# Converting eight weight tiles in pairs and squaring 24 units in pairs, with a new order of the first stage

## The chip, the core and the metric

One core of a Trainium2 chip. The metric is the device time of one execution in microseconds (us). In every matmul below TensorE (PE) runs at one of two clocks, 1.2 or 2.4 GHz; the profile gives the granted share, where 1.00 is 2.4 GHz.

## The reference

An attention layer feeds two dense layers, all in float32 (the weights arrive as float64):

```python
# attention: 2 batches, 8 heads, 768 positions, head size 64
k_sum = k.reshape(B, H, nb, 32, D).max(axis=3)      # one summary key per block of 32
v_sum = v.reshape(B, H, nb, 32, D).mean(axis=3)
scores_l = scale * q @ k^T, kept where |i - j| < 16, else -1e9
scores_s = scale * q . k_sum + log(32)
a = softmax([scores_l, scores_s]);  attn = a @ [v, v_sum]
# 1536 tokens, 512 wide
h = x @ w_in;   x = relu(h)**2 @ w_out              # w_in 512x2048, w_out 2048x512
h = x @ w_in2;  g = h if h>=1, 0 if h<=-1, else (h+1)**2/4;  out = g @ w_out2
```

## The kernel before

Every engine's program is written out by hand. `PLAN` is one string of words such as `H0`, `dq1` or `wh1a`; each word is a step, a number and, where there is a choice, an engine (`a` ScalarE = ACT, `v` VectorE = DVE, `g` GpSimd = POOL). The steps are emitted in that order, so each engine runs its own steps in the order in which they stand in the string, and a step that waits holds up everything behind it on its engine. SyncE (SP) issues all loads, also in the string's order.

Attention is cut into 24 pieces, `S0` to `S23` (a piece is 256 query rows of two heads). For a piece: `S` (PE, L611) multiplies queries with the 96 near keys and the 24 block maxima, which `km` (DVE, L599) makes of a loaded key tensor (`kl`, L582); `M` (DVE, L619) adds the mask and finds the largest; `E` (ACT, L625) is the exponential; `Q` and `R` (DVE, L628, L632) are sum and reciprocal; `N` (L637, POOL or DVE) scales; `T` (PE, L642) transposes, into banks 5 to 7 and later into bank 7 alone; `to` (L645) copies out; `O` (PE, L653) multiplies with the values; `oh` and `ol` (L662, L666) write the result as a high and a low float32r half, `xh` and `xl`. `v`, `vk`, `f` and `vf` make and place the block means of the values.

The weights come as float64. `wl` (L203) loads a tile of 128x512 of them as pairs of 32-bit words; `dl`, `dq` (ACT, L209, L214), `dr`, `ds`, `dt` (DVE, L216 to L220) and `da` (POOL, L223) rebuild a float32 high part `fx` and a rest `fr` from the words; `wh` (L237) rounds `fx` to the high half and `wo` (L242) subtracts to get the low half. Tiles 0, 1 and 4, 5 are `w_in`, tiles 2, 3 and 6, 7 are `w_out` of the first group.

The first group of the first dense layer (four blocks of 128 hidden columns) is done in 24 units `H0` to `H23`, one per block of 256 tokens and hidden block. `H` (PE, L282) is 12 matmuls into half a bank; `ha` (L348, L350) is the relu, `hb` (ACT, L361) the square, `hh` (L373) the high half, `hl` (L377) the low half; `Y` (PE, L409) is 12 matmuls with `w_out` that add into the output banks, which `yo` (L420) copies out. Units 0 to 11 all go to the two halves of bank 4 and relu moves them to SBUF (`tm`); units 12 to 23 use the two halves of banks 4 and 3 in place. All other groups (`P...`, `Y24` on, PE L314 and L409) use a scheme of seven block products with 384 columns, whose operand sums are the steps `ua` to `ur` (L498, L524, L526).

```python
def h_bank(n):
    if n < 12:
        return bank[4][:, n % 2 * CH:(n % 2 + 1) * CH]
    return bank[4 - n % 2][:, n // 2 % 2 * CH:(n // 2 % 2 + 1) * CH]
```

Of the kernel before, what the change touches and what calls it, by code (L numbers as in the profile page):

```python
# [66 lines left out]
dr4 S8 dl5 dr5 O4 hb0 M8 T6 hh0a oh4a H1 R7 E8 ol4 N7g M9 to6a O5 ds5 hl0g Q8 T7 oh5a ha1a ol5 S10 to7a dt5 dl4 ds4 O6
wl9 da5 M10 E9 Y0 wl6 wl7 oh6v vf2 E10 R8 ol6 N8g Q9 O7 S11 hb1 Q10 R9 dt4 T8 N9g oh7a ql4 hh1a R10 ol7 H3 wl8 to8a
M11 bl2 wh4a kl7 da4 S12 wh5a E11 T9 M12 N10g H2 km6 E12 wo5g S13 Q11 dq6 hl1v O8 wo4g dq7 R11 ha2v Y1 hb2 dr7 ha3a
hh2a M13 dl6 hl2g H5 hb3 to9v N11g hh3a dl7 ds7 S14 E13 hl3g Q12 T10 H4 dr6 oh8a to10a ol8 R12 M14 N12g T11 ha4a Y2  # L70
Q13 to11a km7 E14 v6 ds6 S15 dt7 ha5a hb4 O9 R13 dt6 hh4a ql5 v7 wh7a Q14 Y3 da6 hb5 bl3 oh9v M15 vl4 da7 H6 ol9 R14
hl4v dq9 wh6v v8 hh5v ha6a O10 N14v hb6 v9 dr9 oh10a H7 ol10 uf0v hl5v v10 hh6v O11 ha7v hl6g wo6v v11 hb7 Y4 N13g
vk7a dq8 vk6v vk4v oh11a vk5a ol11 H8 E15 vf4 wo7g vf3 hh7a Q15 T12 dl9 Y6 to12v ha8a dr8 hl7v T13 R15 ds9 Y7 ds8
to13a ua0v hb8 yo7a N15v O12 ub0v S16 oh12a dt8 S17 uc0g ol12 T14 M16 H9 M17 E16 ug0g Y5 dl8 Q16 yo5a wl10 O13 hh8v
da8 R16 ha9v S19 N16v to14a E17 S18 uh0g T15 M18 H10 hb9 oh13a to15a Q17 E18 dt9 hl8g T16 M19 H11 wl11 to16a ol13 hh9a
R17 N17v O14 hl9g Q18 S21 oh14a ha10a da9 R18 ol14 S20 ui0a O15 E19 M20 uj0g T17 vl5 ha11v Y8 E20 M21 N18g oh15a S23
hb10 ol15 to17a uk0v S22 hh10a O16 LW0 wh9v H13 Q20 oh16a wo9g hb11 R20 E21 ul0v N20g Y9 Q19 wh8a ol16 um0a R19 hh11v
saa2g O17 Q21 T18 wo8v un0g oh17a H14 M22 to18a dq11 hl10v E22 H12 hl11g sab2v ud0a N19g Y10 ol17 ha12a dr11 ha14a
hb12 uo0g dq10 Q22 T19 hb14 Y11 M23 to19a hh12a sac2v yo11a T20 dr10 sad2v Pa0 ha13a R21 R22 N21v E23 N22g O18 hl12
H15 oh18a sh4a ol18 up0g Q23 to20a ds11 hh14a O19 sh5a Y12 ha15a sl5g oh19a hl14 hb13 ol19 ds10 O20 sl4g dl11 T21  # L80
oh20v R23 H18 dt10 dl10 dt11 hb15 to21a H16 N23v wl13 da11 hh13a ol20 wl12 wh10a hl13 O21 hh15a wh11a ue0g hl15 T22
oh21v ha16a Y13 ol21 hb16 wo11v uq0a da10 to22a Y14 ur0v dq13 ha18a dl13 O22 T23 wo10v oh22a dq12 H19 ua1g ol22 to23a
dr12 dl12 ub1g dr13 O23 hh16a H17 oh23a ds12 hl16 ol23 ds13 H20 ha17a uc1v dt12 LS0 ud1a dt13 Y15 ue1g wl14 ha20a hb18
wh12v wl15 hb17 ha19a hh17a Pz0 da12 Pc0 hb19 Ca0v yo15a hl17 uf1v Pb0 da13 ug1v dq14 Pd0 hh18a wo12g H21 hl18 dr14
wh13a Cc0a wo13g H22 ds14 saa3g Y16 sab3v ha22a uh1v hb22 ha24a sac3v ha21v Y17 sad3g hh19a hb20 hl19 sh6a dt14 dq15
H23 sl6g sh7a dr15 ui1a Y18 sl7v hb21 ha23a uj1v dl14 Y19 uk1g wl16 hh21v Vb0 yo19a hh20v da14 hl21 Pf0 hl20 ds15 Y20
ul1v ha25v um1a dt15 dl15 un1g Y21 hh22v hb24 wl17 hb25 uo1v Pe0 wh14v up1g hl22 dq16 hh24v hh25a Pa1 da15 hl24 hb23
hh23a Vc0 Y22 uq1a ha26v ur1g hl23 hb26 hl25 wh15a Y23 dr16 ua2g hh26a Ca1v dq17 hl26 Pd1 ub2v ds16 dt16 Pc1 uc2v
ha28v Pb1 Cc1a dr17 ud2a ds17 yo23a Pg0 ue2g Vb1 hb28 Pf1 uf2g ha27a hh28v wh16a dt17 Pe1 wo14g hb27 hl28 wh17a Y24
hh27a Vc1 hl27 ha30a wo15g ug2v dl16 wl18 Y25 dl17 uh2v ha29a wl19 da17 hb30 da16 Pg1 wo17v Pa2 ha31a hh30a hb31 Y26  # L90
hb29 ui2a hh31a uj2g hh29a hl31 Y27 hl29 uk2g hl30 Ca2a saa4g ul2v Pc2 sab4g ya1 um2a ya0 dq19 un2g Pd2 ya3 sh9a wo16v
# [705 lines left out]
```

## Time and profile before

| | us |
|---|---|
| median of 3 runs (lowest, highest) | 590.32 (587.84, 590.85) |
| the profiled execution | 590.83 |
| its span, first to last instruction | 589.0 |
| PE busy in the span | 572.5 |
| DVE, ACT, POOL busy | 471.0, 375.8, 257.2 |

Busy time is the union of an engine's instructions. PE's ends are modelled, so it can read busy while its pipeline is not full. The chain is the sequence of pieces of work that ended last, followed back from the end; an engine's idle time matters only where it stands on that chain.

### The profile page before, as it was taken

To read this page: it belongs to the slowest core of one execution; us is meant where nothing else is said; L and a number is where in the kernel's file an instruction comes from. 1 tells how busy PE (TensorE), PEld (TensorE's weight loads), DVE (VectorE), ACT (ScalarE), POOL (GpSimd) and SP (SyncE) were. 2 spreads that over 40 slices of the span, in tenths; PEclk is the share of its full clock that TensorE was granted. 3 is DMA by queue.
4 is the path that set the end of the run, shared out by engine and by line. 5 is a ranking of instruction groups with operands and counts; after the bars stand their busy time and mean duration, and the time that the engine had idled before them with its cause. 6 is when DMAs were issued, how large, how long until landed. Compare 5 with 4: busy or idle time off the path is not lost.

```text
span 589.0 us, 11229 instructions
## 1 busy us (share of the span) xinstructions
PE 572.5 (97%) x4272; PEld 531.5 (90%) x4272; DVE 471.0 (80%) x1062; ACT 375.8 (64%) x800; POOL 257.2 (44%) x220
## 2 busy tenths in 40 slices
...
PEclk8888999999999999999999999999999999999999
...
GB/s 336 377 279 288 145 65 92 1 104 76 38 72 75 70 107 83 98 4 118 93 72 30 44 71 2 142 37 108 21 124 0 133 73 51 32 1 1 0 55 160
DMA packets 16529, 54.16 MB, mean 92 GB/s; under 512 B 1724, under 2 KB 2332, under 8 KB 16476
## 3 DMA queue, kind: packets, MB, share of 16 engines
...
q14 instruction: 20, 0.16, 0.1%
...
## 4 chain that ended last, share of the span: by engine, by line
PE 87%; DVE 6%; DMA 4%; ACT 2%; issue 1%; SPq 0%; DVEq 0%; ACTq 0%
PE bank L409 42%; PE bank L314 33%; PE bank L282 5%; DMA raw<-in_wd_dram 3%; PE bank L611 2%; PE bank L653 2%; PE bank L642 1%; PE bank L466 1%; DMA k<-in_kd_dram 1%; DVE s L619 1%; DVE s L637 1%; DVE sm L628 1%; ACT s L625 1%; DVE xl L666 0%; DVE fx L216 0%
## 5 line engine op out<-in xcount | busy, mean ns | idle before, releaser
L223 POOL TENSOR_TENSOR fr<-fx,fr 128x512 uint32<-128x512 uint32 x64 | 85.0, 1338 | 144.6 <-DVE fx L220 95.1
L377 DVE TENSOR_TENSOR gl<-bank,gh 128x384 fp32r<-128x384 f32 (+1 forms) x124 | 65.2, 538 | 16.2 <-ACT gh L373 14.8
L314 PE MATMUL bank<-xh,wih 128*128 128x384 f32 x224 | 75.4, 337 | 0.1
L314 PE MATMUL bank<-xl,wih 128*128 128x384 f32 x224 | 75.1, 335 | 0.0
L409 PE MATMUL bank<-gh,woh 128*128 128x384 f32 (+1 forms) x288 | 66.3, 321 | 0.0
L409 PE MATMUL bank<-gl,woh 128*128 128x384 f32 (+1 forms) x288 | 65.7, 319 | 0.6 <-DVE gl L377 0.6
L409 PE MATMUL bank<-gh,wol 128*128 128x384 f32 (+1 forms) x288 | 65.4, 319 | 0.0
L352 ACT ACTIVATE tm<-bank,bias 128x384 f32<-128x384 f32 x59 | 34.1, 579 | 37.9 <-PE bank L314 25.6
L314 PE MATMUL bank<-xh,wil 128*128 128x384 f32 x224 | 57.1, 335 | 0.0
L314 PE MATMUL bank<-th,wih 128*128 128x384 f32 x168 | 56.7, 337 | 0.1
L314 PE MATMUL bank<-tl,wih 128*128 128x384 f32 x168 | 56.3, 335 | 0.0
L409 PE MATMUL bank<-woh,gh 128*128 128x512 f32 x180 | 55.9, 392 | 0.0
L409 PE MATMUL bank<-wol,gh 128*128 128x512 f32 x180 | 55.9, 391 | 0.0
L409 PE MATMUL bank<-woh,gl 128*128 128x512 f32 x180 | 55.9, 391 | 0.0
L214 ACT ACTIVATE fx<-raw 128x512 f32<-128x512 f32 x64 | 42.5, 668 | 19.6 <-DMA raw<-in_wd_dram 13.4
L369 DVE SCALAR_TENSOR_TENSOR bank<-bank,tm 128x384 f32<-128x384 f32 x64 | 35.5, 560 | 22.4 <-ACT tm L365 15.1
L434 DVE TENSOR_TENSOR acc<-bank,acc 128x384 f32<-128x384 f32 (+1 forms) x81 | 46.7, 601 | 7.3 <-PE bank L409 7.3
L409 PEld LDWEIGHTS bank<-gl,woh 128*128 128x128 f32 x288 | 49.2, 190 | 1.0 <-DVE gl L377 0.9
L373 ACT CAST gh<-bank 128x384 fp32r<-128x384 f32 (+1 forms) x83 | 38.5, 468 | 17.9 <-DVE bank L369 15.3
L409 PEld LDWEIGHTS bank<-gh,woh 128*128 128x128 f32 x288 | 48.9, 189 | 1.0 <-issue 0.4
L409 PEld LDWEIGHTS bank<-gh,wol 128*128 128x128 f32 x288 | 49.4, 191 | 0.0
L209 ACT ACTIVATE fr<-raw 128x512 uint32<-128x512 uint32 x64 | 42.1, 671 | 10.0 <-POOL wil L259 6.5
...
## 6 DMA issues: line engine op xcount, KB each, us to landing
...
```

Source lines behind the costliest of these rows:

```text
L209: A.activation(fr[n % 2], w_raw(n, 0), AF.Copy, scale=2.0 ** -29)
L214: A.activation(f32(x), f32(hi), AF.Abs)
L223: G.tensor_tensor(fr[n % 2], fx[n % 2], fr[n % 2], ALU.add)
L282: PE.matmul(h_bank(n), a, b, start=i == 0, stop=i == len(ops) - 1)
L314: PE.matmul(q_bank(q, role), a, b, start=bool(first and i == 0), stop=i == 5, skip_group_check=not first)
L352: A.activation(a, h, AF.Relu, bias=bias[:, 1:2], scale=-1.0)
L369: V.scalar_tensor_tensor(h, h, 1.0, a, ALU.max, ALU.mult)
L373: cp(e)(hi, h if m else a)
L377: e.tensor_tensor(lo, h if m else a, f32(hi), ALU.subtract)
L409: PE.matmul(ys[j], a, b, start=f == 0 and i == 0 and (n >= 24 or j % 2 == 0), stop=f == GF - 1 and i == 2 and (n >= 24 or j % 2 == 1))
L434: V.tensor_tensor(a, y_bank(g, t, j), a, ALU.add)
L611: PE.matmul(sbank(i, 2 * h + t)[r * 64:r * 64 + 64, 0 if keys else KW:KW if keys else KN], qs[cc % 2][rows, p, j * QT:(j + 1) * QT], b, st ...
```

## The change

Three things. Weight tiles 0 to 7 are converted two at a time: `raw`, `fx` and `fr` become tiles of 1024 columns, and the words `dl`, `dq`, `dr`, `ds`, `dt`, `da` and `wh` with numbers 0 to 3 now mean a pair of tiles (`wo` stays one tile at a time). The 24 units keep their 12 matmuls `H` and `Y` each, but `ha`, `hb`, `hh` and `hl` with numbers 0 to 11 now mean two units with 512 columns, which lie in the two halves of one bank; the pairs of units 0 to 11 all lie in bank 4, the later pairs alternate between banks 4 and 3. And the words of `PLAN` ahead of `Pa2` stand in another order, with some steps on another engine; from `Pa2` on the string is the same, word for word.

```diff
-warm11 kl0 qf0 cl0 kl1 qf1 kl3 wl1 bl0 km0 kl2 wl0 S0 bl1 M0 wl3 E0 km1 S1 ql1 Q0 vl0 M1 wl2 R0 km3 S3 E1 N0g dq1 Q1
+warm11 qf0 kl3 kl0 wl1 kl1 cl0 wl0 qf1 kl2 bl0 km3 ql1 km0 wl2 S0 wl3 km1 S1 bl1 M0 dq0 M1 dl0 S3 dr0 E1 ds0 dt0 E0 km2
...
-        raw = [mp.tile([128, 512, 2], U32, name=f"raw{i}") for i in range(NRAW)]
-        fx = [mp.tile([128, 512], U32, name=f"fx{i}") for i in range(2)]
-        fr = [mp.tile([128, 512], U32, name=f"fr{i}") for i in range(2)]
+        raws = [mp.tile([128, 1024, 2], U32, name="raw0")]
+        fxm, frm = (mp.tile([128, 1024], U32, name=x) for x in ("fx", "fr"))
...
-        gh = [mp.tile([128, TB], F32R, name=f"gh{i}") for i in range(3)]
-        gl = [mp.tile([128, TB], F32R, name=f"gl{i}") for i in range(3)]
-        tm = [mp.tile([128, TB], F32, name=f"tm{i}") for i in range(3)]
+        ghm, glm = (mp.tile([128, 3 * TB], F32R, name=x) for x in ("gh", "gl"))
+        tmm = mp.tile([128, 3 * TB], F32, name="tm")
+        gh, gl, tm = ([x[:, i * TB:(i + 1) * TB] for i in range(3)] for x in (ghm, glm, tmm))
...
         def w_load(n):
-            r = raw[n % (2 * NRAW)] if n < 8 else raw[n % NRAW]
+            r = raws[n // 2 % 2 if n < 8 else 0][:, half(n)]
...
         def w_raw(n, k):
-            return (raw[n % (2 * NRAW)] if n < 8 else raw[n % NRAW])[:, :, k]
+            return raws[n % 2][:, :, k] if n < 4 else raws[0][:, half(n), k]
+
+        def w_tmp(t, n):
+            return t if n < 4 else t[:, half(n)]
 
         def w_low(n):
-            A.activation(fr[n % 2], w_raw(n, 0), AF.Copy, scale=2.0 ** -29)
+            A.activation(w_tmp(frm, n), w_raw(n, 0), AF.Copy, scale=2.0 ** -29)
...
         def w_add(n):
-            G.tensor_tensor(fr[n % 2], fx[n % 2], fr[n % 2], ALU.add)
+            G.tensor_tensor(w_tmp(frm, n), w_tmp(fxm, n), w_tmp(frm, n), ALU.add)
...
         def w_hi(n, e=A):
+            if n < 4:
+                h = w_place(2 * n)[0]
+                cp(e)(h[:, :1024], f32(fxm))
+                return
...
         def h_bank(n):
-            if n < 12:
-                return bank[4][:, n % 2 * CH:(n % 2 + 1) * CH]
-            return bank[4 - n % 2][:, n // 2 % 2 * CH:(n // 2 % 2 + 1) * CH]
+            b = 4 if n < 12 else 4 - n // 2 % 2
+            return bank[b][:, n % 2 * CH:(n % 2 + 1) * CH]
...
-            if n < 24:
-                h = h_bank(n)
-                return h, tm[n % 2][:, :CH] if n < 12 else h, gh[n % 3][:, :CH], gl[n % 3][:, :CH], 0
+            if n < 12:
+                h, ks = bank[4 if n < 6 else 4 - n % 2], half(n)
+                return h, tmm[:, ks] if n < 6 else h, ghm[:, ks], glm[:, ks], 0
...
-                m, hi, lo = 0, gh[n % 3][:, :CH], gl[n % 3][:, :CH]
+                gs = slice(n % 4 * CH, n % 4 * CH + CH)
+                m, hi, lo = 0, ghm[:, gs], glm[:, gs]
...
-        raw += [at.tile([128, 512, 2], U32, name=f"raw{NRAW + i}") for i in range(NRAW)]
+        raws.append(at.tile([128, 1024, 2], U32, name="raw2"))
```

Three places show what the new order moves. The first is the start of ACT's program; before, each conversion step takes one tile (L214, L209, L237), between exponentials (L625):

```order
L625 ACTIVATE s_128<-s_128,sm_137 128x120 x4
L625 ACTIVATE s_129<-s_129,sm_138 128x120 x4
L214 ACTIVATE fx_77<-raw_75 128x512
L209 ACTIVATE fr_79<-raw_75 128x512
L625 ACTIVATE s_131<-s_131,sm_140 128x120 x4
L237 CAST wih_80<-fx_77 128x512
L209 ACTIVATE fr_78<-raw_74 128x512
L214 ACTIVATE fx_76<-raw_74 128x512
L214 ACTIVATE fx_77<-raw_108 128x512
L625 ACTIVATE s_130<-s_130,sm_139 128x120 x4
```

Now two conversions of a pair stand ahead of the first exponential (the exponential is L630 there):

```order
L215 ACTIVATE fx<-raw_74 128x1024
L210 ACTIVATE fr<-raw_74 128x1024
L630 ACTIVATE s_119<-s_119,sm_128 128x120 x4
L630 ACTIVATE s_118<-s_118,sm_127 128x120 x4
L239 CAST wih_77<-fx 128x1024
L630 ACTIVATE s_121<-s_121,sm_130 128x120 x4
L630 ACTIVATE s_120<-s_120,sm_129 128x120 x4
L215 ACTIVATE fx<-raw_98 128x1024
```

So four exponentials instead of three come before ACT turns to the weights a second time, and both tiles of the first pair are through `dq`, `dl` and `wh` by then.

The second place is the first activations on ACT, before with one unit each (L348 relu, L361 square, L373 high half):

```order
L348 ACTIVATE tm_94<-bank_67 128x256
L214 ACTIVATE fx_76<-raw_74 128x512
L645 COPY acc<-bank_70 120x512
L209 ACTIVATE fr_79<-raw_75 128x512
L361 ACTIVATE tm_94<-tm_94 128x256
L373 CAST gh_88<-tm_94 128x256
L662 CAST xh<-bank_69 128x256
```

and now with two units each (L352, L365, L377):

```order
L352 ACTIVATE tm<-bank_67 128x512
L667 CAST xh<-bank_69 128x256
L210 ACTIVATE fr<-raw_74 128x1024
L667 CAST xh<-bank_69 128x256
L365 ACTIVATE tm<-tm 128x512
L650 COPY pt_123<-bank_69 120x512
L377 CAST gh<-tm 128x512
```

Both units of a pair now have to be through PE before the first of the three runs.

The third place is the relu of the second pair, `ha1`, which has moved to DVE (L354, last row but one). Ahead of it stand a `wh` of a pair (L239), a block maximum (L604) and a `wo` that takes its input from POOL's wide add (L247):

```order
L624 ISA s_121,sm_130<-bank_69,cst 128x120
L624 ISA sm_130 128x1
L239 CAST wih_78<-fx 128x1024
L604 TENSOR_REDUCE ks_114<-k_106 128x24
L247 TENSOR_TENSOR wil_80<-fr,wih_78 128x512
L354 TENSOR_SCALAR tm<-bank_67 128x512
L624 ISA s_118,sm_127<-bank_68,cst 128x120
```

Before, DVE's first relu was that of unit 2, and a reciprocal stood ahead of it:

```order
L377 TENSOR_TENSOR gl_92<-tm_95,gh_89 128x256
L632 RECIPROCAL sm_140<-sm_140 128x4
L350 TENSOR_SCALAR tm_94<-bank_67 128x256
L216 TENSOR_SCALAR fx_77<-fx_77 128x512
```

## Rows read from the trace of the kernel before

**Rows 1.** The page's parts 1 and 2: busy time, granted clock by slices of 14.7 us

```profile
PE 572.5 (97%) x4272; PEld 531.5 (90%) x4272; DVE 471.0 (80%) x1062; ACT 375.8 (64%) x800; POOL 257.2 (44%) x220
...
PEclk8888999999999999999999999999999999999999
```

**Rows 2.** Busy time by stretch: length, PE, PEld, DVE, ACT, POOL (instructions), clock, DMA, GB/s

```profile
20.00:40.00 20.00, 15.36 (x294) 13.19 (x287) 16.73 (x74) 18.48 (x50) 11.29 (x10) 0.83 0.94 334
...
0.00:45.64 45.64, 36.32 (x611) 27.45 (x614) 35.68 (x151) 33.01 (x85) 19.69 (x25) 0.85 0.90 331
45.64:84.50 38.86, 37.42 (x560) 34.54 (x560) 29.95 (x110) 25.55 (x66) 19.31 (x16) 0.96 0.50 163
84.50:110.00 25.50, 23.58 (x407) 22.23 (x406) 24.51 (x77) 20.39 (x56) 17.98 (x15) 1.00 0.25 74
110.00:165.40 55.40, 55.40 (x470) 53.64 (x470) 50.42 (x93) 39.11 (x91) 38.70 (x30) 1.00 0.21 70
0.00:165.40 165.40, 152.72 (x2041) 137.85 (x2042) 140.56 (x429) 118.06 (x296) 95.69 (x85) 0.95 0.47 164
```

**Rows 3.** PE's waits from 165.4 us to the end: total, times, longest

```profile
PE bank L409 <- DVE gl L377: 0.6, 1, 0.6
```

**Rows 4.** The chain in order of time (start, length, what), up to 46 us

```profile
6.70 11.45 DMA raw<-in_wd_dram
...
26.39 1.25 ACT s L625 x4
...
33.76 1.17 PE bank L282 x5
...
39.06 1.43 PE bank L282 x12
...
45.02 0.61 PE bank L653 x16
45.64 0.69 PE bank L611 x32
```

**Rows 5.** ACT by shape up to 165.4 us: count, busy, mean ns, idle before

```profile
L625 ACT ACTIVATE s<-s,sm 128x120 f32<-128x120 f32 x96 | 29.7, 389 | 9.4 <-DVE sm L619 9.3
...
L214 ACT ACTIVATE fx<-raw 128x512 f32<-128x512 f32 x18 | 12.0, 673 | 4.6 <-DMA raw<-in_wd_dram 2.2 <-POOL fr L223 1.4 <-issue 1.1
...
L237 ACT CAST wih<-fx 128x512 fp32r<-128x512 f32 x6 | 3.6, 622 | 0.4 <-DVE fx L220 0.4
...
L645 ACT COPY pt<-bank 120x512 f32<-120x512 f32 x17 | 10.0, 586 | 1.6 <-PE bank L642 1.6
...
L361 ACT ACTIVATE tm<-tm 128x256 f32<-128x256 f32 x12 | 5.0, 414 | 3.0 <-DVE tm L350 3.0
...
L524 ACT CAST th<-acc 128x768 fp32r<-128x768 f32 x3 | 2.5, 824 | 0.0
...
L524 ACT CAST th<-tm 128x384 fp32r<-128x384 f32 x4 | 2.1, 516 | 1.4 <-DVE tm L498 1.4
```

**Rows 6.** The same of DVE and of POOL

```profile
L216 DVE TENSOR_SCALAR fx<-fx 128x512 f32<-128x512 f32 x18 | 10.8, 610 | 0.4 <-ACT fx L214 0.4
...
L377 DVE TENSOR_TENSOR gl<-bank,gh 128x256 fp32r<-128x256 f32 x12 | 4.9, 416 | 1.0 <-ACT gh L373 0.9
...
L377 DVE TENSOR_TENSOR gl<-bank,gh 128x384 fp32r<-128x384 f32 x5 | 2.7, 548 | 0.0
...
L223 POOL TENSOR_TENSOR fr<-fx,fr 128x512 uint32<-128x512 uint32 x18 | 24.5, 1368 | 15.4 <-DVE fx L220 12.9 <-ACT xh L662 1.7 <-ACT fr L209 0.8
...
L498 POOL TENSOR_TENSOR acc<-acc,xl 128x768 f32<-128x768 f32 x4 | 7.7, 1933 | 5.6 <-PE bank L653 5.6
```

**Rows 7.** DVE and POOL in order of time, around 67 us and 85 us

```profile
67.41 0.65 DVE L637 TENSOR_TENSOR s<-s,sm 128x480 f32<-128x480 f32 x1
...
86.30 1.89 DVE L637 TENSOR_TENSOR s<-s,sm 128x480 f32<-128x480 f32 x1
...
85.78 1.89 POOL L498 TENSOR_TENSOR acc<-acc,xl 128x768 f32<-128x768 f32 x1
```

More of the change, by code (lines that the diff above doesn't have):

```diff
@@ L67 @@
[L67 to L91, printed above, removed]
@@ L162 @@
-za2 zd2
+warm11 qf0 kl3 kl0 wl1 kl1 cl0 wl0 qf1 kl2 bl0 km3 ql1 km0 wl2 S0 wl3 km1 S1 bl1 M0 dq0 M1 dl0 S3 dr0 E1 ds0 dt0 E0
+km2 da0 wh0a v0 Q1 S2 M3 v1 R1 ql2 M2 E3 S5 N1v vl0 Q0 E2 wo0g Q3 T1 R0 R3 v2 M5 dq1 N3v v3 to1a S7 E5 dr1 vl1 wo1g v4
+T3 Q2 v5 Q5 to3a vk2v M7 N0g S4 vk3a vk0a vk1a dl1 S9 R2 ds1 N2g T0 vf0 M4 f0a to0a cl1 f1a E4 T2 wl5 R5 dt1 O0 N5g
+to2a O1 vf1 E7 S6 Q4 R4 wl4 O2 M6 N4g oh0a kl5 O3 oh2a ql3 wh1v ol2 S8 kl6 da1 oh1a vl2 ol0 E6 T4 wl7 M8 kl4 S10 to4a
+Q7 oh3a O4 wo2g ol1 E8 Q6 T5 R6 ol3 H1 oh4a N6g R7 to5a ol4 Q8 dq2 O5 M9 N7g T6 oh5a M10 H0 wo3g to6a R8 ol5 E10 dr2
@@ new lines @@
+N8g T7 S11 km5 to7a ha0a O6 ds2 T8 vf2 oh6a dl2 ol6 dt2 wl6 O7 oh7a hb0 wl8 ol7 H2 da2 M11 vl4 wh2v kl7 H3 to8a vl3
+hh0a bl2 km4 E9 wl9 wo4v S12 ha1v O8 hb1 M12 hl0g H4 Q9 E12 wo5g Q10 H5 R9 km6 dq3 N9g Q12 E11 Y0 dr3 ha2a ds3 T9 hh1a
+R10 H6 oh8v to9a hl1g ol8 dl3 Q11 O9 R11 R12 N10v S13 N11g T10 dt3 H7 to10a oh9v wh3a da3 M13 T11 ha3a Y2 ol9 to11a
+E13 v6 wo7g hb3 Q13 v7 S14 dq9 wo6g bl3 O10 N12g ql4 v8 R13 M14 Y3 oh10a E14 N13v ol10 km7 v9 O11 hh3a uf0v v10 dq8
+v11 hb2 S15 vk4a Q14 hl3g vk7a Y1 vk5v dl9 oh11a R14 ol11 vk6a dr9 vf3 Y6 hh2v ds9 ql5 hl2v M15 vf4 T12 dt9 Y7 ug0v
@@ new lines @@
+ha30a Y25 ha29v hb30 uh2v wo17v Pg1 Pa2 ha31a hh30a hb31 Y26 hb29 ui2a hh31a uj2g hh29a hl31 Y27 hl29 uk2g hl30 Ca2a
+saa4g ul2v Pc2 sab4g ya1 um2a ya0 dq19 un2g Pd2 ya3 sh9a wo16v dq18 Pa3 Cc2a sac4v dr19 Pb2 sad4g ya2 dr18 uo2g Y28
+ha32v ds18 hb32 hh32a Vb2 sh8v sl9v Pf2 sl8g up2v Pe2 dl18 Y29 ds19 ha33a dt19 hb33 dt18 uq2a hh33a hl32 ur2g wl20
+dl19 Y30 hl33 wh18a Vc2 wl21 da18 Ca3v wh19a ha34v da19 hb34 Y31 wo19g ya5 ya4 Pg2 hh34v wo18g dq21 ya6 hl34 Pd3 ha35v
+dr21 hb35 Pc3 ds21 dq20 ha36v Pb3 dt21 Cc3a hb36 ya7 hh35a Y32 Vb3 dl21 wh21v dr20 dl20 wl23 da21 hh36a hl36 Pe3 ds20
@@ L235, in w_hi @@
         def w_hi(n, e=A):
+            if n < 4:
+                h = w_place(2 * n)[0]
+                cp(e)(h[:, :1024], f32(fxm))
+                return
             h, l, o, c = w_place(n)
-            cp(e)(h[:, o:o + c.stop - c.start], f32(fx[n % 2][:, c]))
+            cp(e)(h[:, o:o + c.stop - c.start], f32(fxm[:, half(n)][:, c]))
         def w_lo(n, e=G):
@@ L241, in w_lo @@
             d = slice(o, o + c.stop - c.start)
-            e.tensor_tensor(l[:, d], f32(fr[n % 2][:, c]), f32(h[:, d]), ALU.subtract)
+            e.tensor_tensor(l[:, d], f32(frm[:, half(n)][:, c]), f32(h[:, d]), ALU.subtract)
         def w_sum(p, k, e=G):
-            a, b = f32(fr[0]), f32(fr[1])
+            a, b = f32(frm[:, :512]), f32(frm[:, 512:])
             lo, hi = slice(0, 256), slice(256, 512)
@@ L253, in s_hi @@
             p, k = divmod(n, 2)
-            cp(e)(wih[p % 3][:, 1280 - k * 512:1792 - k * 512], f32(fr[k]))
+            cp(e)(wih[p % 3][:, 1280 - k * 512:1792 - k * 512], f32(frm[:, half(k)]))
         def s_lo(n, e=G):
```

163 lines of the change are left out of this document (86 added, 77 removed).

## The prediction, made before the changed kernel ran

> **What bounds it now.** I read the page first, then busy time by stretch, then PE's waits, then the chain. PE is busy 97% of the span and its clock is full from about 60 us on [rows 1], so the question is only where PE loses time. From 165.4 us on it waits 0.6 us in all [rows 3]. That is also where `Pa2` starts, and from `Pa2` on both programs are the same word for word, so those 424 us stay as they are and merely begin earlier or later. Up to 165.4 us PE is idle 165.4 - 152.7 = 12.7 us, and its clock is at 0.95 on average, which is worth some 8 us more [rows 2]. **So about 20 us is the most that the change can win.** Of the 12.7 us, 9.3 lie before 45.64 us, 1.4 up to 84.5 and 1.9 in 84.5 to 110; after that there is none [rows 2].
>
> The reader is to see in the chain who sets PE's pace. At 6.70 us a weight load starts that lands at 18.15; then the chain runs through exponentials on ACT (26.39 us is one of them), and from 33.76 us mostly through PE itself [rows 4]. The stretch 20 to 40 us agrees: ACT 18.5 of 20 us, PE 15.4 [rows 2]. So ACT sets the pace in the first third, DVE later: in 84.5 to 110 us it is busy 24.5 of 25.5 us [rows 2].
>
> **The change, part by part.** *Wide conversions on ACT.* A 512-column step takes 0.67 us [rows 5]. A 1024-column one is not in the trace. Two rows give its growth: 516 ns at 384 columns and 824 at 768, 0.80 ns a column [rows 5], so 0.82 + 256 x 0.80 = 1.03 us at the least; at the most it is twice 0.67 = 1.35, nothing saved. I take 1.10, near the wide rows. The activations of two units (512 columns) cost 0.60, like the 512-column copy (0.586), against 2 x 0.41 [rows 5].
>
> *ACT's work ahead of `O7`.* I take `O7` as a common mark, since PE has done nearly the same before it (12 instead of 11 `S`, one `T` more, no `Y0`; 0.5 us less in all). In ACT's order stand ahead of it: one `E` fewer, 1.24 us (29.7 us for 24 pieces); 6 wide conversions for 12 narrow ones, 8.1 - 6.6 = 1.5; one wide `wh` of 1.05 for four of 0.62, 1.4 (the other pair's has gone to DVE); one wide activation for four narrow steps, 1.0; one copy more, -0.6; the rest -0.1 [rows 5]. Sum: **4.4 us less on ACT.**
>
> *What may not arrive.* ACT now begins with `dq0`, which needs two weight tiles; before, the exponentials of pieces 0 and 1 came first. And `dq1` waits for the fourth tile, which is now behind 5888 KB of loads instead of 5376; at the 331 GB/s of this stretch [rows 2] that is some 1.6 us later than 18.15, so about 19.7. Ahead of `dq1` ACT has work for 2.2 + 5.0 + 1.05 us from about 10 us on, so it is idle some 1.5 us at 18 us; before, the chain too waited for this tile. I put 0.6 us of that against the 4.4, since the chain before waited for this tile as well. Behind it, up to `to4`, which `H1` stands behind, lie 12 us of ACT work (four `E`, four copies, one `dl`, small ones): `H1` starts at about 33.5 us. Up to `to7` another 6.5 us: `O7` ends near 41 against 45.6 (45.02 + 0.61 [rows 4]), with 0.5 us less done. **Stage 1: -3.5 to -4; I take -3.8.** The cover of this sum is that DVE does not take over: its work ahead of `O7` falls too, by about 3 us (one `Q`, one `km`, one `N` fewer, 9 wide for 17 narrow steps).
>
> *From there to `Pa2`.* PE has the same work, 114 us in both. DVE gets lighter by pairing: 24 conversion steps of 0.61 us (less where POOL is quiet) become 12 wide ones, and 30 activation steps of 0.42 become 15 of 0.69 (0.416 at 256 columns, 0.548 at 384, so 1.03 ns a column [rows 6]): together -4 to -7 us. But the new order gives it 26 steps which POOL and ACT had (high halves of `O`, operand sums, low halves) and takes 11 away; at 0.42 to 0.95 us a step that is some +14 - 8 = +6 to +8. So DVE's work up to `Pa2`, 140.6 us of 165.4 [rows 2], changes by -3 to +4, while the time for it gets shorter. The 1.9 us that PE lost in 84.5 to 110 may go (the units' steps there are half as many); against it, a new wait of about 2 us at the second pair (rival C's place). **Stage 2: 0, between -4 and +6.** POOL loses 15 steps; nobody on the chain waits for it, so that counts only through the next point.
>
> *DVE against POOL.* A scaling step `N` takes DVE 0.65 us at 67.41 and 1.89 us at 86.30, where a POOL sum runs from 85.78 to 87.67 [rows 7]. The Trainium skill, "SBUF — State Buffer", section "Who interferes with whom", says that DVE and POOL share one port pair and that whoever comes second is blocked for the whole instruction of the other; the trace agrees, 0.65 against 1.89 us. A wide POOL add is not in the trace; from 1368 ns at 512 columns and 1933 at 768 it is about 2.5 us, at the most 2.74 [rows 6]. Four of these hold DVE longer at a time, but 10 us in place of 11; with 15 POOL steps fewer this speaks for the lower end of DVE's -3 to +4.
>
> **The sum**, against the profiled execution's 590.8 us (the median of the runs is 590.3): -3.8 + 0 + 0 gives 587.0.
>
> **Rivals.** *B, the relief is hidden or given back:* ACT waits for weights as much as it saves, or DVE, without slack in 45 to 165 us, returns the 4 us. For it: DVE was busy 24.5 of 25.5 us in 84.5 to 110 [rows 2] and gets up to 4 us more. Against it: PE never waited after 110 us although DVE was busy 50.4 of 55.4 [rows 2]. Time: 590.8 - 3.8 + 3 = 590.
>
> *C, the one bank of the first pairs:* slower. Pairs 0 to 5 all lie in bank 4, so the next pair's `H` waits until the relu of the last one has read both halves. The relu of pair 1 is on DVE behind a `wo` that needs POOL's wide add; DVE has 40 us of steps ahead of it, so it comes at 45 to 46 us, while PE could be through `H3`, `S12` and `O8` (0.69 and 0.61 [rows 4]) at about 44. That is the 2 us above. If this repeats at `H2`, `H4`, `H6` and `H8` and the clock, which was at 0.83 in 20 to 40 us when PE was idle a quarter of the time [rows 2], falls there as well (an `H` of 1.43 us [rows 4] then takes twice that, three of them +4.3), the stage gives back 4 x 2 + 4.3 = 12: 590.8 - 3.8 + 12 - 2 = 597; half of it gives 593. It decides from about 1.6 us a pair. The Trainium skill, "Perfetto Trace Analysis", section "Optimizing Scalar/DVE Operations", speaks for this case: larger operations help a saturated engine, but where an engine is not saturated and makes others wait, breaking up instructions may let work end sooner. ACT is at 64% over the span but at 92% in 20 to 40 us, so by the rows the first half of the rule holds there.
>
> *D, more than forecast:* ACT ends the first stage earlier and the low-clock stretches shrink with the gaps: up to half of the 20 us, 581.
>
> **Chances.** Forecast with its own range 584 to 588.5: 0.42; D 0.12; B 0.28; C 0.18. Range 581 to 593: it leaves out the far half of C and of D. A measurement tells about 0.5%, 3 us, from no change: under 587.4 is faster, over 593.3 slower. 0.36 of the forecast's 0.42 and D give faster 0.48; B, the rest of the forecast and 0.02 of C give same 0.36; the rest of C is slower, 0.16.
>
> **What would show it.** Right: `O7` ends near 41 us and `H1` starts near 33.5; a wide `dq` near 1.1 us, a wide `da` near 2.5; `Pa2` starts at 161 to 162 us and from there 424 us remain; ACT busy about 105 us up to `Pa2`. Wrong: `O7` not before 44 us (B: look at ACT's wait for `raw`); `O7` early but `Pa2` at 165 (B: DVE on the chain in 60 to 160 us); PE idle or at half clock ahead of `H4` and `H6` (C).

## The result, and the profile after

The changed kernel takes 596.28 us (median of 4 runs, 594.24 to 598.09) against 589.66 of the kernel before, measured beside it: 1.0115 times as long, 95% interval 1.009 to 1.014. Forecast were 587.0 us and faster. The profiled execution takes 596.14 us, 5.3 more than the one before.

Marks on PE split this: `O7` starts at 45.34 us (before 44.95), `Pa2` at 169.38 (before 165.38), and from `Pa2` to the end of the span 424.8 us pass (before 423.7). So stage 1 gives +0.4, stage 2 +3.6, the rest +1.2. By the prediction's own count PE has 0.5 us less to do ahead of `O7` now, so for equal work stage 1 is some 0.9 us late and stage 2 adds some 3.1.

Parts 1 and 2 of the page of the changed kernel:

```profile
PE 571.4 (96%) x4272; PEld 529.0 (89%) x4272; DVE 470.5 (79%) x1051; ACT 365.8 (62%) x750; POOL 243.9 (41%) x205
...
PEclk8699999999999999999999999999999999999999
```

Busy time by stretch, columns as in [rows 2]; the fourth stretch ends where `Pa2` starts:

```profile
0.00:45.64 45.64, 34.16 (x625) 25.11 (x627) 33.13 (x139) 29.40 (x69) 19.29 (x22) 0.81 0.87 312
45.64:84.50 38.86, 36.71 (x609) 33.46 (x606) 36.49 (x112) 25.80 (x64) 22.76 (x16) 1.00 0.57 197
84.50:110.00 25.50, 24.03 (x359) 22.90 (x357) 18.57 (x77) 17.84 (x46) 16.39 (x14) 1.00 0.18 54
110.00:169.40 59.40, 56.25 (x460) 54.03 (x460) 52.40 (x94) 35.07 (x71) 24.52 (x20) 1.00 0.21 72
0.00:169.40 169.40, 151.14 (x2041) 135.49 (x2042) 140.59 (x418) 108.11 (x246) 82.95 (x70) 0.95 0.47 163
```

Against [rows 2] the reader sees that the work did fall where it was meant to: up to `Pa2` ACT has 108.1 us instead of 118.1 and POOL 83.0 instead of 95.7. DVE has 140.6, exactly as before, because the new order handed it steps of the other two. Yet PE is idle 18.3 us instead of 12.7. Of the 5.6 us more, 2.2 lie before 45.64 us (11.5 instead of 9.3) and 3.2 after 110 us, where there was no idle time. From 110 us to `Pa2` pass 59.4 us now, with 460 matmuls, and 55.4 before, with 470: there `Pa2` loses its 4 us. The mean granted clock up to `Pa2` is 0.95 in both, but not stretch by stretch: it is lower in the first 45.64 us (0.81, before 0.85) and higher in the next 38.86 (1.00, before 0.96).

The shares of the chain of waits, first of the kernel before, then of the changed one, show that less of the chain is PE itself and twice as much is DVE:

```profile
PE 87%; DVE 6%; DMA 4%; ACT 2%; issue 1%; SPq 0%; DVEq 0%; ACTq 0%
```

```profile
PE 77%; DVE 12%; ACT 5%; DMA 2%; issue 2%; POOL 1%; SPq 0%; DVEq 0%; ACTq 0%; POOLq 0%
```

**Stage 1.** The start of ACT in order of time, before:

```profile
0.74 1.28 ACT L625 ACT_TABLE_LOAD   x1 [0.74 <-PEq L786]
7.53 1.25 ACT L625 ACTIVATE s<-s,sm 128x120 f32<-128x120 f32 x4 [5.50 <-DVE sm L619]
```

and changed:

```profile
11.37 1.28 ACT L215 ACT_TABLE_LOAD   x1 [11.37 <-DMA raw<-in_wd_dram]
12.66 1.12 ACT L215 ACTIVATE fx<-raw 128x1024 f32<-128x1024 f32 x1
13.69 1.13 ACT L210 ACTIVATE fr<-raw 128x1024 uint32<-128x1024 uint32 x1
14.73 1.52 ACT L630 ACTIVATE s<-s,sm 128x120 f32<-128x120 f32 x5
```

The load of the activation table stands with the first activation. Before, it ran at 0.74 us, when ACT had nothing else to do. Now the first activation is the conversion of a pair; it needs two transfers, and the table load stands behind one of them. It runs at 11.37 us, in the way. The chain after, from there on:

```profile
3.54 7.76 DMA raw<-in_wd_dram
11.37 1.28 ACT L215
12.66 1.13 ACT fx L215
13.82 0.71 DVE fx L217
14.55 0.70 DVE fx L219
15.28 1.23 DVE fx L221
16.51 0.86 DVE ks L604
17.37 0.56 DVE sm L633
18.16 1.55 ACT s L630 x5
```

ACT is busy 29.4 of the first 45.64 us (before 33.0), but it did not leave the chain: of the chain's pieces between 6.7 and 45.6 us, ACT has 9.6 us (before 8.1), and DVE has 12.0 us instead of 3.6, among them the three wide steps one behind the other that the rows show. ACT got less to do, and DVE became the engine that the most of this chain lies on.

**Stage 2.** The largest of PE's waits from 46 to 170 us (total, times, longest):

```profile
PE bank L658 <- DVE xl L671: 2.0, 3, 1.0
PE bank L318 <- DVE bank L325: 1.5, 1, 1.5
PE bank L616 <- DVE ks L604: 0.9, 1, 0.9
```

Two of these and a third one in order of time, on PE:

```profile
83.70 0.65 PE L647 MATMUL bank<-cst,s 128*120 128x128 f32 x4 [0.34 <-POOL s L642]
...
98.75 0.69 PE L658 MATMUL bank<-pt,vw 120*64 120x64 f32 x16 [1.00 <-DVE xl L671]
...
157.82 0.45 PE L318 MATMUL bank<-xh,wih 128*128 128x384 f32 x1 [1.54 <-DVE bank L325]
```

The first waits for `N14`, which stands behind two of POOL's adds:

```profile
80.19 2.51 POOL L224 TENSOR_TENSOR fr<-fx,fr 128x512 uint32<-128x512 uint32 x2 [7.44 <-DVE fx L221]
82.65 0.99 POOL L642 TENSOR_TENSOR s<-s,sm 128x480 f32<-128x480 f32 x1
```

The last waits for `Ca1` (L325), a copy that stands on DVE behind the low half of an operand sum, a weight's low half and another operand sum for later products:

```profile
155.67 0.55 DVE L531 TENSOR_TENSOR tl<-tm,th 128x384 fp32r<-128x384 f32 x1
156.14 0.69 DVE L247 TENSOR_TENSOR wol<-fr,woh 128x512 fp32r<-128x512 f32 x1
156.74 0.55 DVE L503 TENSOR_TENSOR tm<-xh 128x384 f32<-128x384 f32 x1
157.21 0.56 DVE L325 COPY bank<-bank 128x384 f32<-128x384 f32 x1
```

Before, `Ca1` ended at 153.67 and `Pd1`, the matmul that needs it, started at 153.83 with no wait. No single wait of this stage is over 2 us; they are many and short.

**From `Pa2` on** the program is the same, and PE's waits were to be those of [rows 3]. After:

```profile
PE bank L318 <- ACT bank L325: 0.6, 1, 0.6
PE bank L414 <- DVE gl L381: 0.6, 1, 0.6
```

One wait more, 0.6 of the 1.2 us.

**Prices.** ACT's wide conversion, POOL's wide add and DVE's low half of two units, up to `Pa2`:

```profile
L215 ACT ACTIVATE fx<-raw 128x1024 f32<-128x1024 f32 x4 | 4.5, 1135 | 0.0
```

```profile
L224 POOL TENSOR_TENSOR fr<-fx,fr 128x1024 uint32<-128x1024 uint32 x4 | 10.0, 2495 | 20.1 <-DVE fx L221 15.3 <-ACT xh L667 3.6 <-ACT pt L650 1.2
```

```profile
L381 DVE TENSOR_TENSOR gl<-bank,gh 128x512 fp32r<-128x512 f32 x6 | 4.1, 685 | 1.8 <-ACT gh L377 1.8
```

They are 1.14, 2.50 and 0.69 us; 1.10, 2.5 and 0.69 were forecast. So the wide prices held. What was wrong is what a wide conversion was compared with. The forecast took two narrow ones as 2 x 0.67 = 1.35 us, but 0.67 us is the length of each, and one starts before the other has ended. e3_narrow, the run below that gives out two narrow steps for each wide one, shows the two together:

```profile
0.75 1.28 ACT L222 ACT_TABLE_LOAD   x1 [0.75 <-PEq L814]
11.50 1.22 ACT L222 ACTIVATE fx<-raw 128x512 f32<-128x512 f32 x2 [9.47 <-DMA raw<-in_wd_dram]
12.62 1.24 ACT L214 ACTIVATE fr<-raw 128x512 uint32<-128x512 uint32 x2
```

Two narrow ones take 1.22 and 1.24 us, a wide one 1.12 and 1.13: a pair saves ACT 0.1 us and not 0.25. Up to `Pa2` the pairs as a whole save ACT 3.2 us (111.61 us busy in e3_narrow, 108.45 in e1_table, which has the same order). The rest of ACT's 10 us came from the order, which gave its steps to others.

### The profile page after: what moved, and what is told of

The parts are those of the page before. It is cut to its first block, busy times and chain, and to the rows that moved or that the text cites. A ratio compares the mean times of both kernels' runs of the same rounds, so it can differ in the third digit from the quotient of the medians.

```text
span 594.2 us, 11146 instructions
## 1 busy us (share of the span) xinstructions
PE 571.4 (96%) x4272; PEld 529.0 (89%) x4272; DVE 470.5 (79%) x1051; ACT 365.8 (62%) x750; POOL 243.9 (41%) x205
## 4 chain that ended last, share of the span: by engine, by line
PE 77%; DVE 12%; ACT 5%; DMA 2%; issue 2%; POOL 1%; SPq 0%; DVEq 0%; ACTq 0%; POOLq 0%
PE bank L414 38%; PE bank L318 32%; PE bank L286 2%; DMA raw<-in_wd_dram 2%; PE bank L471 1%; DVE fx L217 1%; PE bank L658 1%; PE bank L647 1%; DVE gl L381 1%; DVE s L624 1%; PE bank L616 1%; ACT s L630 1%; DVE fx L221 1%; DVE wil L247 1%; DVE fx L219 1%
## 5 line engine op out<-in xcount | busy, mean ns | idle before, releaser
L224 POOL TENSOR_TENSOR fr<-fx,fr 128x512 uint32<-128x512 uint32 (+1 forms) x60 | 83.6, 1405 | 169.0 <-DVE fx L221 111.3
L381 DVE TENSOR_TENSOR gl<-bank,gh 128x384 fp32r<-128x384 f32 (+1 forms) x118 | 64.4, 558 | 21.1 <-ACT gh L377 19.6
L215 ACT ACTIVATE fx<-raw 128x512 f32<-128x512 f32 (+1 forms) x60 | 41.7, 699 | 21.7 <-DMA raw<-in_wd_dram 17.8
L373 DVE SCALAR_TENSOR_TENSOR bank<-bank,tm 128x384 f32<-128x384 f32 x64 | 35.4, 560 | 22.2 <-ACT tm L369 14.9
L377 ACT CAST gh<-bank 128x384 fp32r<-128x384 f32 (+1 forms) x79 | 38.1, 487 | 17.3 <-DVE bank L373 15.2
L221 DVE SCALAR_TENSOR_TENSOR fx<-raw,fx 128x512 uint32<-128x512 uint32 (+1 forms) x60 | 46.5, 783 | 0.4
## 6 DMA issues: line engine op xcount, KB each, us to landing
acc<-in_vb_dram SPq DMA_DIRECT2D x2, 512.0 KB, 11.5
```

The source lines that it names most:

```text
L215: A.activation(f32(x), f32(hi), AF.Abs)
L221: V.scalar_tensor_tensor(x, hi, 0xC0000000, x, ALU.bitwise_and, ALU.bitwise_or)
L224: G.tensor_tensor(w_tmp(frm, n), w_tmp(fxm, n), w_tmp(frm, n), ALU.add)
L373: V.scalar_tensor_tensor(h, h, 1.0, a, ALU.max, ALU.mult)
L377: cp(e)(hi, h if m else a)
L381: e.tensor_tensor(lo, h if m else a, f32(hi), ALU.subtract)
```

## The experiments

The first four runs ask which part of the change costs the time. The theories: the front of the program starts late (F); the steps that the new order gave to DVE hold up stage 2 (D); the pairs themselves are the harm (P). `O0` starts at 30.8 us in the changed kernel and at 26.0 before, which is what F goes by.

**The table load, e1_table.** A tiny activation stands first in ACT's program:

```diff
+        A.activation(bias[:, 3:4], bias[:, 1:2], AF.Abs)
```

> The changed kernel with one tiny activation on ACT ahead of everything, so that the activation table (1.28 us) is loaded at about 1 us and not behind the landing of the weight pair at 11.37 us. Theory F (the 4.8 us by which O0 is late, 30.8 against 26.0 us, come from what stands at the head of ACT's queue, and all that the wide steps save later only makes up for it): ACT's first conversion at 11.4 in place of 12.7 us, O0 1.0 to 1.3 us earlier, the whole 1.0 to 1.3 us shorter (595.0). Theory D (the time is lost after O7, because the new order loads DVE): O0 earlier as well, but the end within 0.4 us, since DVE gives it back.

594.99 us (10 runs), 1.0086 (1.0049 to 1.0123) times the kernel before, as theory F had it. Its ACT in order of time:

```profile
0.75 1.28 ACT L190 ACT_TABLE_LOAD   x1 [0.75 <-PEq L792]
...
10.90 1.13 ACT L216 ACTIVATE fx<-raw 128x1024 f32<-128x1024 f32 x1 [8.66 <-DMA raw<-in_wd_dram]
...
12.98 1.24 ACT L631 ACTIVATE s<-s,sm 128x120 f32<-128x120 f32 x4
```

The profiled execution is 1.9 us ahead of the changed kernel's at `O7` (43.46) and 1.9 at `Pa2` (167.46): what stage 1 gains arrives whole at the end. In the medians it is 1.3, which the intervals alone don't separate from nothing. Stage 2 stays 124.0 us, as in the changed kernel. Of the later variants all have this line but e3_narrow, e4_dve, h2_oldorder and g4_before_moves. Of these only e4_dve loads the table late (at 10.94 us): h2_oldorder and g4_before_moves begin with exponentials, and e3_narrow's first activation waits for one tile only and has its table at 0.75 us.

**The front, e2_front.** The old order of the loads, and the first two exponentials ahead of the first wide conversion:

```diff
-qf0 kl3 kl0 wl1 kl1 cl0 wl0 ... M0 dq0 M1 dl0 S3 dr0 E1 ds0 dt0 E0
+kl0 qf0 cl0 kl1 qf1 kl3 wl1 wl0 ... M0 E0 ... M1 E1 ... S3 dq0 dl0 dr0 ds0 dt0
```

> As e1_table, and the first loads and the first steps of pieces 0, 1 and 3 in the order of the kernel before: k0, q0, the constants and k1 ahead of k3 and the weights, and the exponentials of pieces 0 and 1 ahead of the first wide conversion. Theory F: first exponential at about 7.5 us and not 14.7, O0 at 26.5 to 28 us and not 30.8, lag kept up to the end: 3 to 4 us shorter than the changed kernel (592 to 593.3). Theory D: O0 earlier, the end at most 1 us earlier (595.3 or more). Theory K (what counts is TensorE's half clock from 9.1 to 26.2 us, whatever the order): the half clock stays as long and O0 comes less than 1.5 us earlier.

596.78 us (6 runs), 1.010 (1.0065 to 1.0134); `O7` at 44.24, later than in e1_table. Neither the order of the loads nor the late start of the exponentials is what stage 1 loses.

**The pairs alone, e3_narrow.** The changed order, buffers and banks, but each wide step as two narrow ones, for instance

```diff
-            A.activation(w_tmp(frm, n), w_raw(n, 0), AF.Copy, scale=2.0 ** -29)
+            for o, i in parts(n, w_tmp(frm, n), w_raw(n, 0)):
+                A.activation(o, i, AF.Copy, scale=2.0 ** -29)
```

> The changed kernel's order and buffers, but every wide step is given out as two narrow ones one behind the other (512 columns in place of 1024, 256 in place of 512), so that only the pairing is undone. Theory P (the wide steps are the harm: the first half is ready later): 1 to 3 us shorter than the changed kernel (593 to 595). Theories F and D: ACT gets some 10 us more work up to Pa2 and DVE some 4 more, so the start is as late and the regained 5 us between T0 and O7 are lost: 3 to 6 us longer (599 to 602).

598.69 us (4 runs), 1.0145 (1.0087 to 1.0203): 2.4 us above the changed kernel. But e3_narrow has its table early, as the rows under "Prices" show, so like is compared with like against e1_table: 3.7 us more, with intervals that overlap a little. `O7` starts at 44.24 us (e1_table: 43.46; the clock of the first 45.64 us is 0.85 in both). So the pairs are worth 0.8 us at `O7` at the most (e3_narrow's first weights also landed 0.6 us later, at 11.50 against 10.90) and some 3.7 in all. Their width is not the harm, and undoing DVE's wide steps does not bring `O7` forward. The other half of this comparison matters more: without any wide step the new order and its buffers are 8.6 us slower than the kernel before. The expectations below that speak of 2.4 us for the pairs rest on the first comparison.

**DVE's new steps, e4_dve.** 22 steps go back to the engine that they had before:

```diff
-yo7v yo15v uq0v ui1v oh13v ... saa2v sl4v ue0v un0v up0v ...
+yo7a yo15a uq0a ui1a oh13a ... saa2g sl4g ue0g un0g up0g ...
```

> The changed kernel with 22 steps ahead of Pa2 given back from DVE to the engine that had them before (12 operand sums and low halves to POOL, ten copies and high halves to ACT), nothing else. Theory D: DVE busy up to Pa2 falls from 140.6 us by some 12, the waits for DVE in 117 to 158 us go, Pa2 starts at 165.5 to 167.5 us in place of 169.4 and the whole is 2 to 4 us shorter (592 to 594). Theory F: everything as before within 0.5 us, since the 4.8 us of the start are carried through. A third way: POOL and ACT are now late where DVE was, and Pa2 stays or gets later by up to 2 us.

594.60 us (9 runs), 1.0086 (1.0058 to 1.0114). Up to `Pa2` DVE is relieved from 140.6 to 129.3 us:

```profile
0.00:168.20 168.20, 151.31 (x2040) 135.14 (x2041) 129.28 (x394) 112.90 (x258) 98.64 (x82) 1.00 0.48 164
```

In the profiled executions PE is 1.0 us ahead of the changed kernel at `O7`, 3.1 at `H22` (135.7 against 138.8 us) and 1.2 at `Pa2` (168.21). The first 1.0 us is not the relief, since all 22 steps stand behind `O7`. It shows what the clock is worth there: up to `O7` both programs are the same, with the table late, and e4_dve ran this stretch at full clock, the changed kernel at 0.81:

```profile
0.00:45.64 45.64, 35.26 (x637) 26.05 (x638) 34.10 (x140) 30.08 (x71) 19.38 (x23) 1.00 0.88 310
```

So the low clock explains at most 1.0 us of stage 1. Behind `O7` the relief wins 2.1 us up to `H22` and has lost 1.9 of them at `Pa2`: the wait of 1.5 us for `Ca1` is still there, and two new ones for ACT (0.7 and 0.5 us) have come. DVE's load alone does not set stage 2.

**Is it the order?** Four runs mix the orders. h2_oldorder takes the whole order of the kernel before, with pairs; a wide step stands where the later of its two narrow steps stood. h1_S17 and h1_O12 keep the new order up to that word, then the old one; r1_S17 is the reverse. The words around `H20` in h2_oldorder and before:

```diff
-hl16 ol23 ds13 H20
+uq0a ur0v hl8 H20
```

> All of the change's pairs, but every step in the order of the kernel before and on its engines: a wide step stands where the later one of its two narrow steps stood. Theory O (the new order loses the time; the pairs themselves are worth some 2.4 us, as the narrow variant of the changed kernel showed): 586 to 589 us, the first exponentials near 10 us as before, TensorE no further behind its work at 160 us than in the kernel before. Theory W (a wide step holds its engine twice as long, and others wait behind it whatever the order): over 592 us.

> The changed kernel's order up to S17 (near 76 us) with the activation table loaded early, and from there the old order and the old engines, with the pairs. Theory O: TensorE is 3 us ahead of the kernel before at S17 and then loses only the 3.2 us that the old order loses up to 160 us, so 586 to 589 us. Rival theory L (the lead at S17 is borrowed: the new order put VectorE's and GpSimd's steps off, and they are paid for after S17 in any order): 591 to 595 us.

> As h1_S17, but the change to the old order comes at O12, some units of work earlier. Theory O: 586 to 589 us, too. Theory L: between the old order's time with pairs and that of h1_S17.

> The reverse: pairs throughout, the old order and engines up to S17, then the changed kernel's order and engines. Theory O: TensorE loses some 8 us between S17 and 160 us, as in the changed kernel, so 594 to 598 us. Theory L: the old start leaves nothing put off, so 587 to 590 us.

618.77 us (1.047, 1.0438 to 1.0502), 611.80 (1.036), 609.05 (1.032) and 602.24 (1.0193). Theory O failed in all four; h2_oldorder is where theory W had it, over 592 us, and the other three fit none. Of h2_oldorder's waits the largest is this, on PE and then on DVE:

```profile
153.52 0.58 PE L286 MATMUL bank<-xh,wih 128*128 128x256 f32 x1 [5.11 <-DVE gl L381]
```

```profile
151.87 1.00 DVE L531 TENSOR_TENSOR tl<-acc,th 128x768 fp32r<-128x768 f32 x1 [2.64 <-ACT th L529]
152.79 0.68 DVE L381 TENSOR_TENSOR gl<-bank,gh 128x512 fp32r<-128x512 f32 x1
```

`H20` writes the bank in which pair 8 lies, and that bank is free only when the low half of both its units (`hl8`, L381) has been read out; `hl8` stands behind `ur0` (L531), which waits for `uq0` on ACT; before, `hl16` alone freed that half and did not. So this one place costs 5.1 of h2_oldorder's 28.5 us; the same wait is in h1_S17 and h1_O12. The others are shorter (2.4 us at most), and PE's clock is 0.86 from 110 to 165 us, where it was full before. Pairs do not fit the old order: a pair holds its bank until the later unit is done. With pairs the new order is 22 us faster than the old one, so it could not simply have been left away. In it `H` (L286) waits 0.5 us for the relu of a pair in all.

Together the runs give four corners: old order without pairs 590.1 us, new order without pairs 598.7, new order with pairs 595.0 (both with the table early), old order with pairs 618.8.

**Can the order be mended?** f1_queues, f2_all and f3_narrow_all take another order of the words up to about 168 us, found by chaining the measured durations: every engine in order, a step after what it reads. Their diffs are the string itself, of which the starts show the kind (e1_table, then f1_queues and f2_all):

```diff
-warm11 qf0 kl3 kl0 wl1 kl1 cl0 wl0 qf1 kl2 bl0 km3 ql1 km0 wl2 S0
+warm11 qf0 kl3 kl0 km0 wl1 kl1 km1 cl0 wl0 km3 qf1 kl2 dq0 bl0 ql1
+cl0 kl1 km1 kl3 km3 kl0 km0 wl1 qf0 wl0 qf1 warm11 S1 kl2 M1 S0
```

> The changed kernel with the activation table loaded early (as e1_table), with its pairs, its engines and TensorE's order kept word for word: only the order of the steps within VectorE's, ScalarE's and GpSimd's own queues up to 168 us is another, chosen by chaining the durations of e1_table's trace so that fewer steps stand ahead of one that TensorE waits for. Theory Q (what the new order loses is steps that stand ready behind others in an in-order queue; the amount of work is no limit): up to 11 us less than e1_table's 595 by that chaining, which leaves out the clock and contention, so 582 to 589 us and TensorE's lag at 160 us 17 to 24 us, where e1_table has 28. Rival P (VectorE's work itself, 140 us busy of 169, sets the first stretch): 593 to 597 us, as e1_table.

> As f1_queues, with TensorE's and the transfers' order free too, still with the changed kernel's pairs and engines. Theory Q: 3 to 4 us less than f1_queues, so 578 to 586 us. Rival P: 593 to 597 us.

> The kernel before, without any pair, with its engines kept and the order of all its steps up to 165 us chosen in the same way from its own trace. If the pairs are worth 2.4 us in a good order too, as e3_narrow showed in the changed kernel's order, this stays 2 us or more above f2_all: 581 to 588 us. If the order alone makes the difference between the kernels (theory Q without a worth of the pairs), it is level with f2_all within 0.4%: 576 to 586 us. By rival P it stays at 589 to 592 us.

All three missed: 606.74, 610.13 and 605.37 us, 1.025 to 1.034 times the kernel before. The traces show one thing that the chaining had left out. Of f2_all, one of PE's waits:

```profile
PE bank L617 <- DVE xl L672: 1.6, 1, 1.6
```

It is a score matmul (L617, `S10`) that waits for `ol4` (L672). It reads nothing of it; the two use different columns of one bank. The program hands a bank on whole: whoever touches it next, in the order of the string, waits for the engine that touched it last, wherever in the bank. The Trainium skill, "PSUM — Partial Sum Buffer", section "PSUM bank collisions raise a hardware error", states that as a rule for synchronizing: by bank (in each 32 partitions), not by address, reads against reads included; these 1.6 us agree with it. f1_queues was to gain up to 11 us on e1_table, but its `Pa2` came at 183.1 us against 167.46 there. The bank rule need not be all of it: its clock was 0.74 up to 45.64 us and 0.73 from 84.5 to 110, where e1_table has 0.85 and 1.00.

**With banks handed on whole: g1_moves, g2_search, g3_narrow.** g1_moves moves 14 single steps ahead in ACT's and DVE's queues, three of them:

```diff
-sh5a ... E23 ... ha6a ... hb7 ... E22
+E22 sh5a ... E23 ... ha6a ... hb7
-M20 ... hh5v Q19 T17 ol15
+ol15 M20 ... hh5v Q19 T17
-N22v ol20
+ol20 N22v
```

> e1_table's kernel with 14 single steps of ScalarE and VectorE moved ahead of 1 to 8 others that stood before them in their queue, each where a step that TensorE waits for stood behind ones that it does not wait for (E22 ahead of hb7, ha6a, E23 and sh5a; ol15 ahead of Q19, hh5v and M20; ol20 ahead of N22v; and so on). Nothing else differs. Theory S (what the new order loses between S17 and the end of the first stretch is the sum of many short waits in in-order queues and at banks that pass from engine to engine in the program's order): chaining e1_table's durations, with each bank handed on whole and in that order, gives 5 us less than e1_table, so 588 to 592 us. Rival P (VectorE's work sets the stretch): 593 to 597 us.

> The changed kernel's pairs and engines with the table loaded early; the order of all steps up to 165 us searched with e1_table's durations, this time with each bank handed on whole between engines in the program's order, which f2_all's search had left out (a matrix product that writes one part of a bank waits for the reader of another part). Theory S: 16 us less than e1_table by that chaining, half of it if contention and the clock take their part, so 578 to 588 us. If the bank rule is not what f1_queues and f2_all lost by, it comes out above 600 us as they did.

> The kernel before, without pairs, engines kept, its order searched in the same way as g2_search, from its own durations. Chaining gives 7 us less than the kernel before: 581 to 589 us, and above g2_search by 2 us or more if the pairs are worth something in a good order.

g1_moves: 592.88 us (12 runs), 1.005 (1.0028 to 1.0072), 2.1 us below e1_table, just outside theory S's 588 to 592. The intervals overlap, but g5_moves36 and g7_relief below, which hold the same moves, come out as low. g2_search: 594.35 (1.0079, 1.0049 to 1.011), 16 us below f2_all, the same search without the bank rule (it also weighted the durations a little differently). So the bank rule is likely most of what f2_all lost by, though the two orders differ in more than that, and g2_search's own range is missed too. g3_narrow, without pairs, 599.38 (1.0151), is 9.5 us slower than the order it began from: what the chaining calls better is not yet faster.

**Are such moves a saving that any kernel has? g4_before_moves** does to the kernel before what g1_moves did, again 14 steps:

```diff
-ol12 T14 M16
+M16 ol12 T14
-wo8v un0g oh17a H14 M22
+M22 wo8v un0g
```

> The kernel before, no pairs, its engines and transfers as they were, with 14 single steps of ScalarE, VectorE and GpSimd moved ahead in their queues, found at its own chain of waits in the way that g1_moves' were. Theory S: chaining gives 4 us less, and g1_moves got 2 of 5, so 586 to 589 us. If then g1_moves is still 3 us or more above it, the new order's loss is not only queue places of that kind, and the pairs' kernel stays behind at equal care. If short queue waits are no part of the time: 589 to 591 us.

589.17 us (12 runs), 0.9993 (0.9971 to 1.0015): no gain, and by the interval at most 1.7 us. So such moves are not a saving of this size in any order, which speaks for the 2.1 us of g1_moves being time that the new order lost.

**More of them, and DVE once more.** g5_moves36 moves 20 more steps, g7_relief gives 12 steps of DVE back on top of g1_moves:

```diff
-oh18a dr11 yo5a
+yo5a oh18a dr11
-ua2v dq16 Ca1v
+Ca1v ua2v
```

```diff
-yo7v oh13v oh14v oh15v oh17v oh19v saa2v sl4v sl5v ue0v un0v up0v
+yo7a oh13a oh14a oh15a oh17a oh19a saa2g sl4g sl5g ue0g un0g up0g
```

> g1_moves with 20 more such moves of single steps in ScalarE's and VectorE's queues (among them Ca1v, for which TensorE waits 1.1 us at Pd1 in g1_moves' trace, ahead of ua2v; Q23, Q18, E15 and E18 ahead of steps for later units). Chaining gives 9 us less than e1_table, of which g1_moves got 2 of 5. Theory S: 588 to 591 us, level with the kernel before. If moves of this kind have no more to give and the last 3 us are VectorE's work or the first stretch: 592 to 594 us, as g1_moves.

> g1_moves with 12 steps between 75 and 130 us given back from VectorE to the engine that they had in the kernel before: yo7, oh13, oh14, oh15, oh17 and oh19 to ScalarE; saa2, sl4, sl5, ue0, un0 and up0 to GpSimd. Theory P2 (once the queue places are mended, VectorE's work is what holds the end of the first stretch: it is busy 94% of 110 to 165 us in g1_moves, 91% in the kernel before): TensorE gains 2 to 3 us on g1_moves by 160 us, so 589 to 591 us. If VectorE is no limit, or the steps come as late on their old engines (in e4_dve 2 us were won by 145 us and lost again by 158): 592 to 595 us.

593.25 us (1.006, 1.0035 to 1.0084) and 592.70 (1.0055, 1.0034 to 1.0077), both as g1_moves. g7_relief shows that giving back these 12 steps does not win the rest; whether DVE's load is no limit, or the steps come as late on the other engines, it does not separate. g5_moves36 does not settle the queue places, because one of its own moves made a new wait. It put `km4` ahead of `ol6` on DVE, and `km4` (L605) waits for a key tensor that is still on its way:

```profile
44.58 0.95 DVE L605 TENSOR_REDUCE ks<-k 128x24 f32<-128x768 f32 x1 [3.54 <-DMA k<-in_kd_dram]
45.45 0.41 DVE L672 TENSOR_TENSOR xl<-bank,xh 128x256 fp32r<-128x256 f32 x1
```

```profile
PE bank L659 <- DVE xl L672: 4.3, 1, 4.3
```

The second view is PE's waits from 38 to 47 us: PE waits 4.3 us for `ol6` ahead of `O7`, where e1_table's waits 0.5, and `O7` starts at 45.92 us (e1_table: 43.46). From `O7` to `Pa2` the same trace takes 120.2 us, as the kernel before (120.4) and 3.8 less than e1_table. So the further moves did bring stage 2 back in that execution, and `km4` took the gain in stage 1. g5_moves36 with `km4` in its old place was not run.

About 3 us above the kernel before stay in the best of these versions. **That part is open**, and this trace says where to look first. No version with pairs that was run is as fast as the kernel before.

## Why the prediction was wrong

- **Stage 1, forecast -3.8, measured +0.4 at `O7`**, some +0.9 for equal work. Three steps of the prediction failed. "What may not arrive" put 0.6 us against the 4.4 that ACT was to win, and the cover of the sum was "that DVE does not take over". But ACT's first instruction waits for two tiles until 11.37 us and has the table load behind that wait; without it (e1_table) `O7` starts 1.9 us earlier, which is 1.5 before the old `O7`, some 1.0 for equal work. And DVE did take over: its work fell as forecast (33.1 us for 35.7 in the first 45.64), yet it has 12.0 us of the chain there instead of 3.6. The third is the size of "wide conversions on ACT": a pair saves 0.1 us and not 0.25. The 1.5 us for six of them are then some 0.6, and all that the pairs bring at `O7` is 0.8 us at the most (e3_narrow against e1_table). ACT's work did fall, by 3.6 us for the forecast 4.4, but by the order more than by the pairs, and the sum took this difference of work for a difference of time. Of the forecast 3.8 us some 2.8 never came, even with the table early. Neither late exponentials and the order of the loads (e2_front) nor DVE's wide steps (e3_narrow) keep them back, and the clock accounts for 1.0 us at the most (e4_dve); what does is open.
- **Stage 2, forecast 0 (-4 to +6), measured +3.6**, some +3.1 for equal work. The range held it, and DVE's work changed by 0.0 (forecast -3 to +4, though its two parts add up to -1 to +4). That PE would lose 3.2 us after 110 us, where it had lost none, was foreseen nowhere; the argument against rival B, "PE never waited after 110 us", was taken from an order that no longer stood. g1_moves and g4_before_moves speak for part of it (2.1 us) being places in the queues. The 114 us of PE work are 116.4 by [rows 2]; the sum does not use them.
- **From `Pa2`, forecast 0, measured +1.2.** An identical program is not an identical time: the engines enter it in another position, and one wait of 0.6 us was added.
- **Rivals.** The time lies above B's 590, outside the stated range, and between C's 593 and 597. C's number came near by luck: its mechanism (the next `H` held up by the relu of a pair in the one bank, PE at half clock) did not act, since the clock is 1.00 from 45.64 us on and `H` waits 0.5 us for a relu. That a pair holds its bank longer is real, though: in h2_oldorder it costs 5.1 us at one place, there by the low half and not by the relu. Rival B comes nearest ("`O7` not before 44 us: look at ACT's wait for `raw`" was its sign, and that wait is there), with the price too small. The page "Perfetto Trace Analysis" of the Trainium skill, section "Optimizing Scalar/DVE Operations", was called on for C: breaking up instructions may end sooner on an engine that is not saturated. These runs do not bear that out: e3_narrow, which breaks them up in the same order, is 3.7 us slower than e1_table. What cost was the order, 8.6 us without any pair.
